# Decode attention with grouped heads on one core: 8 MB loads with 64 KB rows, K transposed in place, and the last V slots with V as stationary operand

## The chip, the cores and the metric

The kernel runs on one core of one Trainium2 chip. The metric is device microseconds (us) of one execution, lower is better; a verdict of "same" means within 2%.

Engine names in the profile: PE is TensorE (matmuls), PEld its weight loads, DVE is VectorE, ACT is ScalarE, POOL is GpSimd, SP is the engine whose queue issues the large loads (SPq is its sequencer). The granted clock is the share of TensorE's full clock that a profile records as allowed. L121 is line 121 of the kernel's source.

## The reference

One query token attends to 65,536 keys, with 32 query heads that share 8 key/value heads of width 128, all in bf16:

```python
B, Hq, Hkv, Sq, Sk, D = 1, 32, 8, 1, 65536, 128
k = jnp.repeat(k, rep, axis=1)          # rep = 4 query heads per K/V head
scores = jnp.einsum("bhqd,bhkd->bhqk", q, k) * D ** -0.5
p = softmax(scores, axis=-1)
out = jnp.einsum("bhqk,bhkd->bhqd", p, v)
```

K and V are 134 MB each and every byte is used once, so 268.4 MB must come in from memory. The order of the keys does not matter as long as K and V use the same one.

## The kernel before

For each of the 8 groups it loads K in four pieces of 4 MB, transposes each in blocks on DVE, multiplies with the queries on PE, takes the softmax, then loads V in four pieces of 4 MB and accumulates. K and V pieces share four buffers of 4 MB. In a piece each of the 128 partitions gets 128 keys ("slots"), which are 32 KB in a row of HBM.

```python
SL = 128; NB = 4                                   # slots per partition, pieces per group
iop = tc.tile_pool(name="iop", bufs=4)             # four 4 MB buffers
ktp = tc.tile_pool(name="ktp", bufs=3)             # transposed parts of K

def load(src, g, b, parts, name):
    t = iop.tile([P, SL, D], bf16, name=name, tag="io")
    view = src[0, g, b * KEYS:(b + 1) * KEYS, :].rearrange("(p t) d -> p t d", p=P)
    for lo, hi in parts:
        nc.sync.dma_start(out=t[:, lo:hi, :], in_=view[:, lo:hi, :])
    return t

# scores: 32 slots at a time
kt = ktp.tile([P, TS * D // 2], u32, name="kt")
nc.vector.transpose(out=kt[:, :], in_=kn[:, t0:t0 + TS, :] ... )     # cut
# eight matmuls of 512 columns on kt per 32 slots                      # cut

# the last piece of V (cut): comes in parts, its last 32 slots one by one
cut = [(0, 64), (64, 96), (96, 112), (112, 120), (120, 128)]
...
for t in range(96, 128):
    nc.tensor.matmul(out=fin[:, :], lhsT=et[:, b, o:o + H], rhs=vt[:, t, :], ...)
```

In the last loop the probabilities (4 columns) are the stationary operand, which a weight load (PEld) puts into PE first (`lhsT`), and V (128 columns) is the moving one (`rhs`), which is then multiplied with it.

## Time and profile before

| | before |
|---|---|
| median time, us (3 runs, 634.33 to 635.99) | 635.89 |
| profiled span, us | 634.2 |
| share of the span: PE, DVE, DMA queue of the large loads | 60%, 56%, 98.7% |
| a group of heads (33.55 MB), K landing to K landing, us | 77.8 |
| first data packet starts, last one ends, us | 1.76, 628.55 |
| last packet's end to the end of the span, us | 5.68 |

First, lines of the page of the kernel before. In the DMA line each digit is the busy share of the 16 DMA engines in one fortieth of the span, in tenths; below it what they moved. The q1 line gives packets, MB, and the share of the span that the packets took. The last two lines are groups of instructions: count, busy us, mean ns, idle time before them and what ended it.

```profile
span 634.2 us, 4903 instructions
...
DMA  8999999999999999999999999999999999999995
GB/s 366 430 436 433 437 434 432 429 430 429 432 430 431 430 429 432 430 429 430 429 430 430 429 432 431 432 435 430 428 431 432 427 432 430 429 432 431 434 423 217
...
q1 hardware_dynamic: 9944, 268.44, 98.7%
...
L121 PE MATMUL sc<-kt,wz 128*128 128x512 bf16 x1024 | 274.4, 426 | 139.1 <-DVE kt L112 139.0
L112 DVE STREAM_TRANSPOSE kt<-kn 128x2048 uint32<-128x2048 uint32 x128 | 284.4, 2278 | 23.7 <-DMA kn<-in_k_dram 23.7
```

No slice between the first and the last shows a pause of the DMA engines; PE and DVE wait. The same for two groups, from the windows view (window in us, length, busy us of each engine with its count of instructions, then PE's granted clock, DMA share, GB/s):

```profile
170.18:248.01 77.83, 46.95 (x263) 18.13 (x263) 43.85 (x33) 2.90 (x8) 0.00 (x0) 0.79 1.00 431
248.01:325.96 77.95, 45.01 (x263) 17.45 (x263) 43.97 (x33) 2.90 (x8) 0.00 (x0) 0.81 1.01 431
```

In 78 us PE works 46 and DVE 44, the DMA engines all of it. The chain of waits of the kernel before (share by line; then start and length of two pieces) must be read with that in mind:

```profile
by line: PE sc L121 31.7%; DMA kn<-in_k_dram 26.3%; DVE kt L112 20.6%; issue 6.5%; PE vacc L179 3.7%; DMA vt<-in_v_dram 3.4%; DMA q_in<-in_q_dram 1.3%; DVE mx L134 1.0%; ACT e L158 0.9%; DVE et L162 0.8%; PE fin L224 0.6%; PE pb L148 0.4%; 
...
381.08 24.00 DMA kn<-in_k_dram
405.10 2.32 DVE kt L112
```

It gives more than half of the span to PE and DVE, because it steps from a load back to the issue of that load, and from there to the work that freed its buffer. But a load that takes 9.7 us at 431 GB/s was issued 24 us before it landed: it stood in the queue most of that time. The work that freed its buffer could have been some 14 us later without costing anything (an estimate, 24.0 less 9.7).

The end of the kernel before, PE's instructions in time (start, busy us, line, operation, in brackets the idle time before):

```profile
623.96 1.04 PE L179 MATMUL vacc<-vt,et 128*16 128x512 bf16 x16 [3.02 <-DMA vt<-in_v_dram]
626.46 1.02 PE L179 MATMUL vacc<-vt,et 128*8 128x256 bf16 x16 [1.46 <-DMA vt<-in_v_dram]
627.71 2.72 PE L224 MATMUL fin<-vt,et 128*4 128x128 bf16 x24 [0.23 <-DMA vt<-in_v_dram]
630.22 0.63 PE L229 MATMUL fin<-vs,sel 128*4 128x128 f32 x2
630.65 1.06 PE L224 MATMUL fin<-vt,et 128*4 128x128 bf16 x8
```

The last part of V landed at 628.99 us; PE was then still busy with slots that had come earlier and ended 2.7 us later, at 631.71.

### The profile page before, as it was taken

What the parts mean: (1) busy time and instruction counts of PE and PEld (TensorE: products, weight loads), DVE (VectorE), ACT (ScalarE), POOL (GpSimd) and SP (SyncE); (2) the same over time, 40 slices, a digit from 0 to 9 for tenths busy, and PEclk for the clock granted to TensorE, in tenths of its full rate; (3) what the DMA queues carried; (4) which work ended last, traced back from release to release, by engine and by line L of the source; (5) the groups of instructions that cost most, each with busy time, mean ns of one, the idle gap of its engine ahead of it and who ended that gap; (6) DMA issues with size and microseconds to landing.
All of it is one profiled execution on the core that took longest, in us unless ns stands there. A gap on an engine that the chain in (4) does not pass through costs nothing.

```text
span 634.2 us, 4903 instructions
## 1 busy us (share of the span) xinstructions
PE 377.9 (60%) x2136; PEld 149.0 (23%) x2136; DVE 356.1 (56%) x291; ACT 24.5 (4%) x65; POOL 5.0 (1%) x7
## 2 busy tenths in 40 slices
PE   0876528864387644767357674576735677455865
PEld 0232203321132211322113221122211223122323
DVE  3886128761377704886057860578506785067841
ACT  0000100001000100001000010000100001000010
POOL 3000000000000000000000000000000000000000
PEclk9898767898679875988759877598865977769787
DMA  8999999999999999999999999999999999999995
GB/s 366 430 436 433 437 434 432 429 430 429 432 430 431 430 429 432 430 429 430 429 430 430 429 432 431 432 435 430 428 431 432 427 432 430 429 432 431 434 423 217
DMA packets 10213, 268.78 MB, mean 424 GB/s; under 512 B 1360, under 2 KB 1360, under 8 KB 1744
## 3 DMA queue, kind: packets, MB, share of 16 engines
q1 hardware_dynamic: 9944, 268.44, 98.7%
q8 instruction: 16, 0.26, 0.2%
q10 hardware_dynamic: 248, 0.04, 0.0%
q14 instruction: 5, 0.04, 0.0%
HBM read 268.47 MB, written 0.01 MB: 423 GB/s over the span
## 4 chain that ended last, share of the span: by engine, by line
PE 37%; DMA 31%; DVE 24%; issue 6%; ACT 1%; ACTq 0%; SPq 0%; DVEq 0%
PE sc L121 32%; DMA kn<-in_k_dram 26%; DVE kt L112 21%; PE vacc L179 4%; DMA vt<-in_v_dram 3%; DMA q_in<-in_q_dram 1%; DVE mx L134 1%; ACT e L158 1%; DVE et L162 1%; PE fin L224 1%; PE pb L148 0%; DVE m L140 0%; PE pt L138 0%; DVE wz L100 0%; DVE nrow L144 0%
## 5 line engine op out<-in xcount | busy, mean ns | idle before, releaser
L121 PE MATMUL sc<-kt,wz 128*128 128x512 bf16 x1024 | 274.4, 426 | 139.1 <-DVE kt L112 139.0
L112 DVE STREAM_TRANSPOSE kt<-kn 128x2048 uint32<-128x2048 uint32 x128 | 284.4, 2278 | 23.7 <-DMA kn<-in_k_dram 23.7
L121 PEld LDWEIGHTS <-wz 128*128 128x128 bf16 x1024 | 107.6, 105 | 305.1 <-issue 214.5
L179 PE MATMUL vacc<-vt,et 128*16 128x512 bf16 (+1 forms) x1024 | 90.5, 519 | 88.8 <-DMA vt<-in_v_dram 73.9
L191 DVE TENSOR_TENSOR vm<-vacc,mask 128x512 f32<-128x512 f32 x8 | 5.5, 692 | 141.6 <-PE vacc L179 141.6
L179 PEld LDWEIGHTS <-et 128*16 128x16 bf16 (+1 forms) x1024 | 34.1, 111 | 134.8 <-issue 108.3
L134 DVE TENSOR_REDUCE mx<-sc 128x1 f32<-128x512 f32 x32 | 22.2, 692 | 74.0 <-PE sc L121 74.0
L158 ACT ACTIVATE e<-sc,nmb 128x512 bf16<-128x512 f32 x32 | 21.7, 683 | 585.0 <-DVE nmb L153 584.1
L162 DVE STREAM_TRANSPOSE et<-e 128x512 bf16<-128x512 bf16 x32 | 22.1, 712 | 8.6 <-ACT e L158 8.6
L239 PE MATMUL fin<-vs,sel 128*4 128x128 f32 x14 | 3.7, 361 | 12.9 <-DVE vs L196 12.9
L196 DVE TENSOR_REDUCE vs<-vm 128x128 f32<-128x512 f32 x8 | 8.2, 1019 | 0.3
L138 PE MATMUL pt<-ident,mg 128*1 128x128 f32 x8 | 2.2, 270 | 7.9 <-DVE mg L136 7.9
L203 DVE TENSOR_SCALAR o<-fin,rl 4x128 bf16<-4x128 f32 x8 | 2.7, 339 | 6.8 <-PE fin L239 4.4
L158 ACT ACTIVATION_READ_ACCUMULATOR e<-sc,nmb 128x1 f32 x32 | 6.2, 194 | 0.0
L148 PE MATMUL pb<-one,nrow 1*128 1x1 f32 x16 | 3.0, 256 | 5.0 <-DVE nrow L144 5.0
L89 DVE STREAM_TRANSPOSE qT<-q_in 128x64 uint32<-128x64 uint32 x1 | 0.2, 245 | 8.8 <-DMA q_in<-in_q_dram 8.8
L239 PEld LDWEIGHTS fin<-vs,sel 128*4 128x4 f32 x14 | 0.6, 84 | 19.2 <-DVE vs L196 19.2
L63 POOL MEMSET wz<- 128x5120 bf16 x1 | 4.4, 4365 | 0.3 <-POOLq L255 0.3
L224 PE MATMUL fin<-vt,et 128*4 128x128 bf16 x32 | 3.8, 310 | 0.2 <-DMA vt<-in_v_dram 0.2
L140 DVE TENSOR_REDUCE m<-pt 1x4 f32<-1x128 f32 x8 | 2.2, 278 | 3.0 <-PE pt L138 3.0
L148 PEld LDWEIGHTS pb<-one,nrow 1*128 1x128 f32 x16 | 2.3, 182 | 6.5 <-DVE nrow L144 6.5
L224 PEld LDWEIGHTS <-et 128*4 128x4 bf16 x32 | 3.4, 126 | 0.8 <-issue 0.5
(25 smaller groups left out, 18.5 us busy)
## 6 DMA issues: line engine op xcount, KB each, us to landing
kn<-in_k_dram SPq DMA_DIRECT2D x31, 4096.0 KB, 32.4
vt<-in_v_dram SPq DMA_DIRECT2D x31, 4096.0 KB, 26.7
kn<-in_k_dram SPq DMA_DIRECT2D x2, 2048.0 KB, 11.9
vt<-in_v_dram SPq DMA_DIRECT2D x1, 2048.0 KB
vt<-in_v_dram SPq DMA_DIRECT2D x1, 1024.0 KB
vt<-in_v_dram SPq DMA_DIRECT2D x1, 512.0 KB, 21.8
vt<-in_v_dram SPq DMA_DIRECT2D x2, 256.0 KB
out_dram<-o ACTq DMA_DIRECT2D x7, 1.0 KB
```

The source lines that it names most:

```text
L63: nc.gpsimd.memset(wz[:, :, :, :, :], 0.0)
L112: nc.vector.transpose(out=kt[:, :], in_=kn[:, t0:t0 + TS, :].rearrange("p t d -> p (t d)").bitcast(u32),)
L121: nc.tensor.matmul(out=sc[:, :], lhsT=wz[:, g, s, w, 28 - 4 * gp:28 - 4 * gp + P], rhs=ktb[:, u:u + 16, s, :, w], start=(n == 0), stop=(n ...
L134: nc.vector.tensor_reduce(out=mx[:, b:b + 1], in_=scs[b][:, :], axis=AX.X, op=ALU.max)
L148: nc.tensor.matmul(out=pb[:, :], lhsT=nrow[:, :, :].rearrange("o x h -> o (x h)"), rhs=one[:, :], start=True, stop=True,)
L158: nc.scalar.activation(out=e[:, :], in_=scs[b][:, :], func=ACT.Exp, bias=nmb[:, :], scale=SCALE, accum_out=ls[:, b:b + 1],)
L162: nc.vector.transpose(out=et[:, b, :], in_=e[:, :])
L179: nc.tensor.matmul(out=vacc[32 * c:32 * c + 4 * ng, 0:ng * D], lhsT=et[:, b, o:o + 4 * ng], rhs=vt[:, :, :].rearrange("p (y t) d -> p y t ...
L191: nc.vector.tensor_tensor(out=vm[:, :, :], in0=vacc[:, :].rearrange("p (y d) -> p y d", d=D), in1=mask[:, :, :], op=ALU.mult,)
L196: nc.vector.tensor_reduce(out=vs[:, :], in_=vm[:, :, :].rearrange("p y d -> p d y"), axis=AX.X, op=ALU.add)
L224: nc.tensor.matmul(out=fin[:, :], lhsT=et[:, b, o:o + H], rhs=vt[:, t, :], start=(t == 96), stop=(t == 127),)
L239: nc.tensor.matmul(out=fin[:, :], lhsT=sel[:, :], rhs=vs[:, :], start=True, stop=True)
```

## The change

The intent is a faster DMA stream: half as many rows, each twice as long. Three 8 MB buffers need 192 KB of each partition, so everything else shrinks: K is transposed inside its own buffer, the query weights are kept for two groups rather than eight (written by GpSimd), a mask becomes a per-partition factor. The last V slots change the roles of their operands so that PE should have less to do after the last landing. The diff, cut:

```diff
-SL = 128
-NB = 4
+SL = 256
+NB = 2
...
-    iop = ctx.enter_context(tc.tile_pool(name="iop", bufs=4))
-    ktp = ctx.enter_context(tc.tile_pool(name="ktp", bufs=3))
+    iop = ctx.enter_context(tc.tile_pool(name="iop", bufs=3))
...
-            kt = ktp.tile([P, TS * D // 2], u32, name="kt")
-            nc.vector.transpose(
-                out=kt[:, :],
-                in_=kn[:, t0:t0 + TS, :].rearrange("p t d -> p (t d)").bitcast(u32),
-            )
+            part = kn[:, t0:t0 + TS, :].rearrange("p t d -> p (t d)")
+            nc.vector.transpose(out=part.bitcast(u32), in_=part.bitcast(u32))
...
-                cut = [(0, 64), (64, 96), (96, 112), (112, 120), (120, 128)]
-                for t in range(96, 128):            # V moving, 32 slots
...
+    cuts = [0, 128, 192, 224, 240, 248, 256]
+    vs = collect()
+    for t in range(192, 240):                       # V stationary, 48 slots
+        nc.tensor.matmul(
+            out=oT[:, :], lhsT=vt[:, t, :], rhs=et[:, 3, o:o + H], start=(t == 192), stop=(t == 239)
+        )
+    nc.vector.tensor_copy(out=oTs[:, :], in_=oT[:, :])
+    nc.tensor.matmul(out=fin[:, :], lhsT=sel[:, :], rhs=vs[:, :], start=True, stop=False)
+    nc.tensor.matmul(out=fin[:, :], lhsT=oTs[:, :], rhs=ident[:, :], start=False, stop=False)
+    for t in range(240, 256):                       # V moving, 16 slots
+        nc.tensor.matmul(
+            out=fin[:, :], lhsT=et[:, 3, o:o + H], rhs=vt[:, t, :], start=False, stop=(t == 255)
+        )
```

More of the change, by code (lines that the diff above doesn't have):

```diff
@@ L14 @@
 D = 128
-SL = 128
-NB = 4
+SL = 256
+NB = 2
+NS = 4
 G = 8
@@ L39 @@
     const = ctx.enter_context(tc.tile_pool(name="const", bufs=1))
-    iop = ctx.enter_context(tc.tile_pool(name="iop", bufs=4))
-    ktp = ctx.enter_context(tc.tile_pool(name="ktp", bufs=3))
-    ep = ctx.enter_context(tc.tile_pool(name="ep", bufs=2))
+    iop = ctx.enter_context(tc.tile_pool(name="iop", bufs=3))
+    ep = ctx.enter_context(tc.tile_pool(name="ep", bufs=1))
     st = ctx.enter_context(tc.tile_pool(name="st", bufs=2))
@@ L47, with load @@
     pfn = ctx.enter_context(tc.tile_pool(name="pfn", bufs=1, space=bass.MemoryType.PSUM))
-    def load(src, g, b, parts, name):
+    def load(src, g, b, cuts, name):
         t = iop.tile([P, SL, D], bf16, name=name, tag="io")
         view = src[0, g, b * KEYS:(b + 1) * KEYS, :].rearrange("(p t) d -> p t d", p=P)
-        for lo, hi in parts:
+        for lo, hi in zip(cuts, cuts[1:]):
             nc.sync.dma_start(out=t[:, lo:hi, :], in_=view[:, lo:hi, :])
         return t
+    first = load(k, 0, 0, [0, SL], "kn")
     q_in = const.tile([P, D], bf16)
@@ L59 @@
         nc.scalar.dma_start(out=q_in[32 * a:32 * a + 32, :], in_=q[0, :, 0, :])
-    first = load(k, 0, 0, [(0, 64), (64, 128)], "kn")
-    wz = const.tile([P, G, 2, 2, WB], bf16)
-    nc.gpsimd.memset(wz[:, :, :, :, :], 0.0)
+    wz = [const.tile([P, 2, 2, WB], bf16, name=f"wz{i}") for i in range(2)]
+    for w in wz:
+        nc.gpsimd.memset(w[:, :, :, :], 0.0)
     ident = const.tile([P, P], fp32)
@@ L67 @@
     nc.vector.memset(one[:, :], 1.0)
-    ones = const.tile([P, 512], fp32)
-    nc.vector.memset(ones[:, :], 1.0)
     sel = const.tile([P, H], fp32)
@@ L82 @@
     )
-    mask = const.tile([P, 4, D], fp32)
-    for y in range(4):
-        nc.vector.tensor_scalar_mul(out=mask[:, y, :], in0=ones[:, 0:D], scalar1=sely[:, y:y + 1])
+    vacc = pva.tile([P, 4, D], fp32)
+    nc.vector.memset(vacc[:, :, :], 0.0)
     qT = const.tile([P, 2, 32], u32)
@@ L94, with weights, scores @@
     )
-    for a in range(4):
-        rows = slice(32 * a, 32 * a + 32)
-        c0 = 28 + 32 * a
-        for s in range(2):
-            for w in range(2):
-                nc.vector.tensor_copy(
-                    out=wz[rows, :, s, w, c0:c0 + H], in_=qTb[rows, s, :, :, w]
-                )
-    vacc = pva.tile([P, 512], fp32)
-    nc.vector.memset(vacc[:, :], 0.0)
-    def scores(g, kn):
+    def weights(g):
+        w = wz[g % 2]
+        for a in range(4):
+            rows = slice(32 * a, 32 * a + 32)
+            c0 = 28 + 32 * a
+            nc.gpsimd.tensor_copy(
+                out=w[rows, :, :, c0:c0 + H],
+                in_=qTb[rows, :, g, :, :].rearrange("p s h w -> p s w h"),
+            )
+        return w
+    def scores(kn, w, t_lo):
         sc = psc.tile([P, 512], fp32, name="sc")
         n = 0
-        for t0 in range(0, SL, TS):
-            kt = ktp.tile([P, TS * D // 2], u32, name="kt")
-            nc.vector.transpose(
-                out=kt[:, :],
-                in_=kn[:, t0:t0 + TS, :].rearrange("p t d -> p (t d)").bitcast(u32),
-            )
-            ktb = kt[:, :].bitcast(bf16).rearrange("p (t s i w) -> p t s i w", s=2, i=32, w=2)
+        for t0 in range(t_lo, t_lo + 128, TS):
+            part = kn[:, t0:t0 + TS, :].rearrange("p t d -> p (t d)")
+            nc.vector.transpose(out=part.bitcast(u32), in_=part.bitcast(u32))
+            ktb = part.rearrange("p (t s i w) -> p t s i w", s=2, i=32, w=2)
             for u in range(0, TS, 16):
-                gp = (t0 + u) // 16
+                gp = (t0 - t_lo + u) // 16
                 for s in range(2):
-                    for w in range(2):
+                    for e in range(2):
                         nc.tensor.matmul(
                             out=sc[:, :],
-                            lhsT=wz[:, g, s, w, 28 - 4 * gp:28 - 4 * gp + P],
-                            rhs=ktb[:, u:u + 16, s, :, w],
+                            lhsT=w[:, s, e, 28 - 4 * gp:28 - 4 * gp + P],
+                            rhs=ktb[:, u:u + 16, s, :, e],
                             start=(n == 0),
@@ L131, in softmax @@
     def softmax(g, scs):
-        mx = st.tile([P, NB], fp32, name="mx")
-        for b in range(NB):
+        mx = st.tile([P, NS], fp32, name="mx")
+        for b in range(NS):
             nc.vector.tensor_reduce(out=mx[:, b:b + 1], in_=scs[b][:, :], axis=AX.X, op=ALU.max)
@@ L153, in softmax @@
         nc.vector.tensor_copy(out=nmb[:, :], in_=pb[:, :])
-        ls = st.tile([P, NB], fp32, name="ls")
-        et = ep.tile([P, NB, 512], bf16, name="et")
-        for b in range(NB):
-            e = ep.tile([P, 512], bf16, name="e")
+        ls = st.tile([P, NS], fp32, name="ls")
+        et = ep.tile([P, NS, 512], bf16, name="et")
+        for b in range(NS):
             nc.scalar.activation(
-                out=e[:, :], in_=scs[b][:, :], func=ACT.Exp, bias=nmb[:, :], scale=SCALE,
+                out=et[:, b, :], in_=scs[b][:, :], func=ACT.Exp, bias=nmb[:, :], scale=SCALE,
                 accum_out=ls[:, b:b + 1],
             )
-            nc.vector.transpose(out=et[:, b, :], in_=e[:, :])
-        pl = pms.tile([H, NB], fp32, name="pl", tag="misc")
+            nc.vector.transpose(out=et[:, b, :], in_=et[:, b, :])
+        pl = pms.tile([H, NS], fp32, name="pl", tag="misc")
         nc.tensor.matmul(out=pl[:, :], lhsT=sel[:, :], rhs=ls[:, :], start=True, stop=True)
@@ L171, with wcol, wide @@
     started = set()
-    def wide(g, b, et, vt, gp0, ng, last=False):
+    def wcol(t):
+        return (t % 16) * 32 + 4 * (t // 16)
+    def wide(g, b, et, vt, t_lo, last=False):
+        bank, gp0 = (b * SL + t_lo) // 128, (t_lo % 128) // 16
+        vv = vt[:, t_lo:t_lo + 64, :].rearrange("p (y t) d -> p y t d", t=16)
         for tt in range(16):
             c = tt % 4
-            key = (g, c)
             o = tt * 32 + 4 * gp0
             nc.tensor.matmul(
-                out=vacc[32 * c:32 * c + 4 * ng, 0:ng * D],
-                lhsT=et[:, b, o:o + 4 * ng],
-                rhs=vt[:, :, :].rearrange("p (y t) d -> p y t d", t=16)[:, gp0:gp0 + ng, tt, :],
-                start=key not in started,
+                out=vacc[32 * c:32 * c + 16, :, :],
+                lhsT=et[:, bank, o:o + 16],
+                rhs=vv[:, :, tt, :],
+                start=(g, c) not in started,
                 stop=last and tt >= 12,
@@ L186, in wide, with collect @@
             )
-            started.add(key)
-    def collect(g):
-        vm = st.tile([P, 4, D], fp32, name="vm")
-        nc.vector.tensor_tensor(
-            out=vm[:, :, :], in0=vacc[:, :].rearrange("p (y d) -> p y d", d=D),
-            in1=mask[:, :, :], op=ALU.mult,
-        )
-        vs = st.tile([P, D], fp32, name="vs")
-        nc.vector.tensor_reduce(
-            out=vs[:, :], in_=vm[:, :, :].rearrange("p y d -> p d y"), axis=AX.X, op=ALU.add
-        )
+            started.add((g, c))
+    def collect():
+        vs = st.tile([P, D], fp32, name="vs")
+        nc.vector.tensor_scalar_mul(out=vs[:, :], in0=vacc[:, 0, :], scalar1=sely[:, 0:1])
+        for y in range(1, 4):
+            nc.vector.scalar_tensor_tensor(
+                out=vs[:, :], in0=vacc[:, y, :], scalar=sely[:, y:y + 1], in1=vs[:, :],
+                op0=ALU.mult, op1=ALU.add,
+            )
         return vs
@@ L205, in finish @@
         store.dma_start(out=out[0, g * H:(g + 1) * H, 0, :], in_=o[:, :])
-    pend = None
     for g in range(G):
+        w = weights(g)
         scs = []
         for b in range(NB):
-            kn = first if (g, b) == (0, 0) else load(k, g, b, [(0, 128)], "kn")
-            scs.append(scores(g, kn))
+            kn = first if (g, b) == (0, 0) else load(k, g, b, [0, SL], "kn")
+            scs.append(scores(kn, w, 0))
+            scs.append(scores(kn, w, 128))
         et, rl = softmax(g, scs)
-        for b in range(NB):
-            if g == G - 1 and b == NB - 1:
-                cut = [(0, 64), (64, 96), (96, 112), (112, 120), (120, 128)]
-                vt = load(v, g, b, cut, "vt")
-                wide(g, b, et, vt, 0, 4)
-                wide(g, b, et, vt, 4, 2, last=True)
-                fin = pfn.tile([H, D], fp32, name="fin")
-                vs = collect(g)
-                for t in range(96, 128):
-                    o = (t % 16) * 32 + 4 * (t // 16)
-                    nc.tensor.matmul(
-                        out=fin[:, :], lhsT=et[:, b, o:o + H], rhs=vt[:, t, :],
-                        start=(t == 96), stop=(t == 127),
-                    )
-                    if t == 119:
-                        nc.tensor.matmul(
-                            out=fin[:, :], lhsT=sel[:, :], rhs=vs[:, :], start=False, stop=False
-                        )
-            else:
-                vt = load(v, g, b, [(0, 128)], "vt")
-                wide(g, b, et, vt, 0, 4)
-                wide(g, b, et, vt, 4, 4, last=(b == NB - 1))
-        if g < G - 1:
-            vs = collect(g)
@@ L238 @@
+        end = g == G - 1
+        for b in range(NB - end):
+            vt = load(v, g, b, [0, SL], "vt")
+            for t_lo in range(0, SL, 64):
+                wide(g, b, et, vt, t_lo, last=(b == NB - 1 and t_lo == SL - 64))
+        if not end:
+            vs = collect()
             fin = pfn.tile([H, D], fp32, name="fin")
             nc.tensor.matmul(out=fin[:, :], lhsT=sel[:, :], rhs=vs[:, :], start=True, stop=True)
-        finish(g, fin, rl)
+            finish(g, fin, rl)
+    g, b = G - 1, NB - 1
@@ new lines @@
+    cuts = [0, 128, 192, 224, 240, 248, 256]
+    vt = load(v, g, b, cuts, "vt")
+    for t_lo in (0, 64, 128):
+        wide(g, b, et, vt, t_lo, last=(t_lo == 128))
+    vs = collect()
+    oT = pms.tile([P, H], fp32, name="oT", tag="misc")
+    for t in range(192, 240):
+        o = wcol(t - 128)
+        nc.tensor.matmul(
+            out=oT[:, :], lhsT=vt[:, t, :], rhs=et[:, 3, o:o + H], start=(t == 192), stop=(t == 239)
+        )
+    oTs = st.tile([P, H], fp32, name="oTs")
+    nc.vector.tensor_copy(out=oTs[:, :], in_=oT[:, :])
@@ L244 @@
+    fin = pfn.tile([H, D], fp32, name="fin")
+    nc.tensor.matmul(out=fin[:, :], lhsT=sel[:, :], rhs=vs[:, :], start=True, stop=False)
+    nc.tensor.matmul(out=fin[:, :], lhsT=oTs[:, :], rhs=ident[:, :], start=False, stop=False)
+    for t in range(240, 256):
+        o = wcol(t - 128)
+        nc.tensor.matmul(
+            out=fin[:, :], lhsT=et[:, 3, o:o + H], rhs=vt[:, t, :], start=False, stop=(t == 255)
+        )
+    finish(g, fin, rl)
 _INS = ['q', 'k', 'v']
```

## The prediction

> **What bounds the kernel now.** The DMA stream. The slice view shows DMA busy at 9 or more in all slices but the first and last, at 430 GB/s; the windows view gives each group of heads (33.55 MB) 77.8 us from 14.6 to 559.2 us, at DMA share 1.00 and 431 GB/s. The Trainium skill, page "DMA: Bandwidth & Descriptors", section "Where 436 GB/s comes from", puts the ceiling at 435.2 GB/s; the trace agrees to 1%. PE (60%) and DVE (56%) have room; the chain of waits names them only because it follows when buffers come free, some 17 us before the queue needs them (issue to landing is 27 to 32 us, a 4 MB load takes 9.7). At the ends: about 2.5 us before the first byte, and some 6 us after the last landing: PE at granted clock 0.50 on the last slots (24 matmuls in 2.72 us from 627.71, two f32 matmuls 0.43, eight matmuls 0.87), the scaling 0.34, the store about 2.4.
>
> **The stream.** Bytes stay. In the trace's packet records a 16 KB row took 611 ns (median) on its DMA engine, a 32 KB row 1216, a semaphore packet 9. So a row costs about 6 ns beside its bytes. Each engine moves 512 rows of 32 KB; with 64 KB rows 256, which saves about 1.5 us, and half the semaphore packets 0.3 us. If a 64 KB row is cut in two, only the 0.3 us remain. Saving: 0.3 to 1.8 us, all on the critical path.
>
> **Do three buffers starve the queue?** Estimate: an 8 MB load takes 19.5 us; load n needs load n-3 consumed within 39 us of landing. K: eight transposes of 2.27 us = 18.2 us on DVE, no longer held up by three kt buffers; PE, at 0.27 us a matmul, ends 2 to 5 us later. So K is free 21 to 24 us after landing; softmax takes 5 us, 8 MB of V 6 us. The tightest slack is about 15 us. In-place transposes wait only for their own region: the trace already shows reads waiting for just their piece (the cut last V load: 619.04, 623.96, 626.46, 627.71). The stream should stay unbroken. Fewer constants, weights on GpSimd, a later first transpose (22 us instead of 13) and q arriving later are off the path.
>
> **The tail.** 48 slots with V stationary, f32 matmuls, then 16 slots in the old form (16 x 0.11 = 1.8 us). Before, 32 in the old form. If a V-stationary slot costs 0.06 us, the end is as before; if 0.11 like the old ones, PE ends about 2.5 us later. I take +0.7 us.
>
> **Sum.** 635.9 - 1.8 + 0.7 = 634.8 us, range 631 to 638.5. Faster by over 2% 0.02, within 2% 0.95, slower by over 2% 0.03. Faster than 623 is nearly excluded: the bytes alone take 617 us at the ceiling.
>
> **What would show it.** Stream: group windows of 77.4 to 77.7 us, DMA share 1.00; 64 KB packets of about 2.43 us, DMA packet count near 5,000. Buffers: SP issues 10 us or more before the running load ends; no slice under 425 GB/s. Tail: from last V landing to the end of the last matmul 3 us before, 3 to 5.5 after.
>
> **What would make it wrong.** A tracker that orders transposes behind matmuls of the same tile (K then takes 38 us and the stream stalls some 18 us per group, over 10% slower); 64 KB packets at another rate; in-place transposes slower than 2.27 us; a much cheaper tail.

## The result, and the profile after

The changed kernel took 633.0 us (median of 4 runs, 632.85 to 633.37), the kernel before 635.31 us (now 4 runs), ratio 0.9966 with a 95% interval of 0.9948 to 0.9983. A ratio is the mean time of one kernel's fast runs over that of the other's of the same rounds, so not quite the ratio of the medians. Three later repeats on three chips gave 0.9950, 0.9955 and 0.9952, by medians 3.1, 2.7 and 3.1 us. So the gain is 2.3 to 3.1 us, 0.3 to 0.5%: small, but clear of the noise.

The page of the changed kernel, the same lines as before:

```profile
span 631.0 us, 4882 instructions
...
DMA  9999999999999999999999999999999999999995
GB/s 400 404 461 420 441 404 457 428 434 453 408 457 407 458 411 450 415 446 428 433 436 428 433 432 429 437 428 437 424 442 420 445 425 440 433 432 429 436 407 231
...
q1 hardware_dynamic: 5336, 268.44, 98.6%
...
L116 PE MATMUL sc<-kn,wz 128*128 128x512 bf16 x1024 | 262.0, 410 | 170.9 <-DVE kn L110 170.6
L110 DVE STREAM_TRANSPOSE kn<-kn 128x2048 uint32<-128x2048 uint32 x128 | 282.5, 2274 | 80.2 <-DMA kn<-in_k_dram 80.2
```

The DMA line has no gap: three buffers are enough. The GB/s line now swings between 400 and 461, which is not a stall: bytes are counted by whole packets, a packet is 64 KB now, and most engines start their packets together (11 of 16 within 0.4 us, from 201.1 us on). The in-place transposes take 2.27 us as the others did. Two groups in the windows view of the changed kernel:

```profile
179.20:256.64 77.44, 44.20 (x263) 17.49 (x263) 43.22 (x35) 2.78 (x8) 0.76 (x4) 0.83 1.00 434
256.64:334.08 77.44, 45.56 (x263) 18.04 (x263) 43.22 (x35) 2.78 (x8) 0.76 (x4) 0.76 1.00 434
```

A group takes 77.44 us where it took 77.83 and 77.95 (most others before 77.8), at the same DMA share of 1.00: the engines are as busy, and get more through. In each of the two profiles one of the six K-to-K intervals is longer by 1.4 us (79.1 before, 78.9 after); what that is stays open, and it is the same on both sides.

The packet records put the whole difference in place:

| from the packet records, us | before | after |
|---|---|---|
| first data packet starts | 1.76 | 1.76 |
| last data packet ends | 628.55 | 625.93 |
| length of the stream | 626.79 | 624.17 |
| from there to the end of the span | 5.68 | 5.10 |
| packet of a 32 KB row, of a 64 KB row, median ns | 1216, - | 1216, 2421 |

Of the 3.2 us between the profiled spans, 2.6 are stream and 0.6 tail. The chain of waits of the changed kernel:

```profile
by line: DVE kn L110 42.0%; DMA kn<-in_k_dram 40.8%; DMA vt<-in_v_dram 5.3%; PE sc L116 4.5%; DMA q_in<-in_q_dram 4.4%; issue 0.8%; PE fin L243 0.3%; PE oT L233 0.2%; ACTq L60 0.2%; DVE vs L192 0.2%; PE vacc L178 0.2%; DVE mx L129 0.1%; PE 
...
2.13 27.97 DMA q_in<-in_q_dram
...
374.00 39.01 DMA kn<-in_k_dram
413.01 0.02 issue
413.03 17.67 DVE kn L110 x8
```

Two things are to be seen. The K load is issued 39 us before it lands and takes 19.4, so the buffer came free some 19 us early. And the four small q loads, 8 KB each, took 28 us (8.5 before): they share the DMA engines with the 8 MB loads, which now hold an engine for 2.4 us per packet. The runs with shorter rows, told below, bear this out, with all else kept: the transpose of q began at 30.2 us here, at 18.1 with 32 KB rows and at 9.4 with 8 KB rows. The late q moved the first transposes to 31 us.

The end of the changed kernel, PE's instructions in time:

```profile
621.34 1.04 PE L178 MATMUL vacc<-vt,et 128*16 128x512 bf16 x16 [0.90 <-DMA vt<-in_v_dram]
623.99 0.59 PE L239 MATMUL fin<-vs,sel 128*4 128x128 f32 x2 [1.61 <-DVE vs L192]
624.51 1.44 PE L233 MATMUL oT<-et,vt 128*128 128x4 bf16 x48
626.21 0.59 PE L240 MATMUL fin<-ident,oTs 128*4 128x128 f32 x2 [0.26 <-DVE oTs L237]
626.59 1.91 PE L243 MATMUL fin<-vt,et 128*4 128x128 bf16 x16
```

The 48 slots with V stationary took 1.44 us, 30 ns each at granted clock 0.50; the 16 old-style slots took 1.91 us, 119 ns each. The last part of V landed at 626.37, so all of the 1.91 us lie behind it, and PE ended 2.1 us after it. The cheap slots hardly depend on the clock: in the run with 32 KB rows below, 48 of them took 1.35 us at granted clock 1.00, 28 ns each.

### The profile page after: what moved, and what is told of

Its sections match the earlier page's. It is cut to its first block, busy times and chain, and to the rows that moved or that the text cites. A ratio compares the mean times of both kernels' runs of the same rounds, so it can differ in the third digit from the quotient of the medians.

```text
span 631.0 us, 4882 instructions
## 1 busy us (share of the span) xinstructions
PE 362.8 (57%) x2154; PEld 145.2 (23%) x2154; DVE 347.3 (55%) x287; ACT 23.6 (4%) x65; POOL 7.9 (1%) x40
## 4 chain that ended last, share of the span: by engine, by line
DMA 51%; DVE 43%; PE 5%; issue 1%; ACTq 0%; SPq 0%; DVEq 0%
DVE kn L110 42%; DMA kn<-in_k_dram 41%; DMA vt<-in_v_dram 5%; PE sc L116 5%; DMA q_in<-in_q_dram 4%; PE fin L243 0%; PE oT L233 0%; ACTq L60 0%; DVE vs L192 0%; PE vacc L178 0%; DVE mx L129 0%; PE fin L239 0%; PE fin L240 0%; DVE vs L190 0%; DVE o L200 0%
## 5 line engine op out<-in xcount | busy, mean ns | idle before, releaser
L116 PE MATMUL sc<-kn,wz 128*128 128x512 bf16 x1024 | 262.0, 410 | 170.9 <-DVE kn L110 170.6
L110 DVE STREAM_TRANSPOSE kn<-kn 128x2048 uint32<-128x2048 uint32 x128 | 282.5, 2274 | 80.2 <-DMA kn<-in_k_dram 80.2
L116 PEld LDWEIGHTS <-wz 128*128 128x128 bf16 x1024 | 104.4, 102 | 326.6 <-issue 195.9
L178 PE MATMUL vacc<-vt,et 128*16 128x512 bf16 x1008 | 88.6, 526 | 46.2 <-DMA vt<-in_v_dram 44.4
L178 PEld LDWEIGHTS <-et 128*16 128x16 bf16 x1008 | 33.9, 116 | 96.6 <-issue 86.1
L152 ACT ACTIVATE et<-sc,nmb 128x512 bf16<-128x512 f32 x32 | 21.5, 685 | 586.7 <-DVE nmb L148 586.7
L156 DVE STREAM_TRANSPOSE et<-et 128x512 bf16<-128x512 bf16 x32 | 21.7, 711 | 7.1 <-ACT et L152 7.1
L99 POOL COPY wz<-qT 32x16 bf16<-32x16 bf16 x32 | 6.1, 190 | 445.5 <-PE sc L116 415.9
L192 DVE SCALAR_TENSOR_TENSOR vs<-vacc,sely,vs 128x128 f32<-128x128 f32 x24 | 8.4, 351 | 0.9
L152 ACT ACTIVATION_READ_ACCUMULATOR et<-sc,nmb 128x1 f32 x32 | 6.5, 203 | 0.0
```

What stands on the lines that cost most here:

```text
L99: nc.gpsimd.tensor_copy(out=w[rows, :, :, c0:c0 + H], in_=qTb[rows, :, g, :, :].rearrange("p s h w -> p s w h"),)
L110: nc.vector.transpose(out=part.bitcast(u32), in_=part.bitcast(u32))
L116: nc.tensor.matmul(out=sc[:, :], lhsT=w[:, s, e, 28 - 4 * gp:28 - 4 * gp + P], rhs=ktb[:, u:u + 16, s, :, e], start=(n == 0), stop=(n == 31),)
L152: nc.scalar.activation(out=et[:, b, :], in_=scs[b][:, :], func=ACT.Exp, bias=nmb[:, :], scale=SCALE, accum_out=ls[:, b:b + 1],)
L156: nc.vector.transpose(out=et[:, b, :], in_=et[:, b, :])
L178: nc.tensor.matmul(out=vacc[32 * c:32 * c + 16, :, :], lhsT=et[:, bank, o:o + 16], rhs=vv[:, :, tt, :], start=(g, c) not in started, stop= ...
```

## The experiments

**Theory.** A row costs about 10 ns on its DMA engine beside its bytes; half as many rows save the 2.6 us of the stream. **Rivals.** (a) The size and number of the loads pays, not the row. (b) The spacing of the rows in HBM matters. (c) The new tail is the gain. (d) Compute or buffers matter, as the chain of waits suggests. The changed kernel ran again beside each set. The edits are shown shortened; text after a `#` in them is a remark or stands for code left out.

> The changed kernel once more, on the same chip as the next three, as their base. Repeats its result: 2.0 to 2.6 us under the kernel before (ratio 0.9959 to 0.9969), 64 KB packets of 2421 ns median, first packet at 1.8 us, last packet ends near 625.9 us.

It took 632.91 us (kernel before 636.05, ratio 0.9950, interval 0.9937 to 0.9964): half a microsecond more gain than I had expected, in the kernel before's time rather than in its own (632.91 against 633.0).

**Rows of 32 KB in one 8 MB load.** Two 32 KB rows per partition from two places, still one load:

```diff
-view[:, lo:hi, :]                                   # "(p t) d -> p t d"
+src[...].rearrange("(h p t) d -> p h t d", h=2, p=P)   # one load, two 32 KB rows per partition
```

> The changed kernel, still one 8 MB load at a time into three buffers, but each load takes its 64 KB per partition as two 32 KB rows from two places of HBM (the keys are only permuted, the result stays right). Theory (the row is what pays: about 10 ns per packet beside the bytes): packets of 32 KB at 1216 ns, about 248 more per engine, so the stream is 248 x 11 ns = 2.7 us longer than the changed kernel's; time 635.5 to 636, level with the kernel before within 0.1% or so once its new tail is counted. Rival (the size and number of loads pays, or the new tail): level with the changed kernel, ratio to before 0.9966.

635.33 us (just under the 635.5 to 636 expected), 2.42 over the changed kernel on the same chip; packets of 1216 ns; the stream 626.52 us, against 624.38 for the changed kernel beside it. Two groups in the windows view of this run:

```profile
102.05:179.84 77.79, 43.87 (x263) 17.46 (x263) 43.22 (x35) 2.78 (x8) 0.76 (x4) 0.83 1.00 431
179.84:257.60 77.76, 45.62 (x263) 17.94 (x263) 43.21 (x35) 2.78 (x8) 0.76 (x4) 0.79 1.00 431
```

The group is back at 77.8 us and 431 GB/s with 8 MB loads, three buffers, in-place transposes and the new tail all kept. Rival (a) falls.

**Two 4 MB loads side by side.** Each load from slot 0 to 128 and 128 to 256:

```diff
-load(k, g, b, [0, SL], "kn")
+load(k, g, b, [0, 128, 256], "kn")                 # V the same
```

> The changed kernel with each 8 MB load issued as two 4 MB loads side by side in the buffer (32 KB rows at a 64 KB pitch). Theory (rows): as with two 32 KB rows in one load, plus 31 more semaphore packets of 9 ns per engine = 0.3 us: 2.9 to 3.2 us over the changed kernel. Rival (number of loads): the whole gain is lost here but not in the run with 32 KB rows in one load. Rival (pitch of the rows in HBM): this one differs from that run by more than 0.3 us.

636.18 us, 3.3 over the changed kernel. The stream is 626.47 us, the same as with 32 KB rows in one load, though the rows lie at another pitch and there are 31 more loads: rival (b) falls, and the 0.3 us I had put on the extra semaphore packets are not to be seen. A group in this run:

```profile
169.91:247.69 77.78, 45.47 (x263) 17.97 (x263) 43.62 (x35) 2.78 (x8) 0.76 (x4) 0.83 1.00 431
```

By the criterion, more than 0.3 us between the two runs, the times alone would have spoken for rival (b), and the estimate of 2.9 to 3.2 us was nearly met for another reason than the one given. The 0.85 us between the two times are in the tail (5.82 against 4.72 us after the last packet). In this run's profile PE's clock was at 0.50 for the last 10 us, in the other's for the last 5. I did not isolate what sets that.

**Rows of 8 KB.** As the 32 KB run, with h=8.

> The changed kernel with one 8 MB load at a time made of 8 KB rows. Theory (a fixed cost per packet): 8 KB packets took 313 ns in the cut last load of the kernel before, so 64 KB take 8 x 313 = 2504 ns in place of 2421; 248 x 83 ns = 20.6 us over the changed kernel, time about 653. Rival (engine rate does not depend on the row, only on load size): within 1 us of the changed kernel.

650.62 us (4 runs), 17.7 over the changed kernel; the estimate was 20.6. Two groups in the windows view:

```profile
184.04:263.72 79.68, 44.50 (x263) 17.65 (x263) 43.22 (x35) 2.78 (x8) 0.76 (x4) 0.78 1.01 421
263.72:343.41 79.69, 44.78 (x263) 17.73 (x263) 43.22 (x35) 2.79 (x8) 0.76 (x4) 0.80 1.01 420
```

The DMA share reads 1.01: recorded packet times overlap a little when packets are short, so summing them counts too much (645.9 us per engine in this run, in a stream of 641.6). The intervals are the safer measure. In a group each engine moves 32 times 64 KB:

| row | K-to-K interval, us | per 64 KB and engine, ns | over the 64 KB row, per extra row, ns |
|---|---|---|---|
| 64 KB | 77.44 | 77.44 / 32 = 2420 | |
| 32 KB | 77.78 | 2431 | 11 / 1 = 11 |
| 8 KB | 79.69 | 2490 | 70 / 7 = 10 |

One cost per row, 10 to 11 ns, fits all three. Single intervals vary (two of six in the first repeat of the changed kernel are 77.8 us), so the whole streams are a second measure: against the mean of four profiles of the changed kernel, 624.17 us, the 32 KB rows cost 9.5 ns each (2.35 us, 248 rows more per engine) and the 8 KB rows 9.9 (17.4 us, 1768 more). Without the row cost 64 KB would take 2410 ns, which on 16 engines is 435 GB/s. The Trainium skill's "DMA: Bandwidth & Descriptors", section "Where 436 GB/s comes from", states 435.2 GB/s as the ceiling; this agrees. The same section says that for loads from HBM the memory side, about 358 GB/s, binds first; here, with one core at work, it did not (434 measured). So, by this fit, the changed kernel's stream is 0.4% from what longer rows could only approach.

**The tail, both ways.** First the second base, then the changed kernel with the old tail, then the kernel before with the new one.

> The changed kernel again, as base of the next three on the same chip: ratio to before 0.9959 to 0.9969.

632.97 us (ratio 0.9955, again a little more gain than expected).

```diff
-    for t in range(192, 240): oT ... V stationary        # and copy, f32 matmul, 16 slots V moving
+    wide over slots 192 to 224; for t in range(224, 256): fin ... V moving
```

> The changed kernel with the old handling of the last 64 slots (two of the four rows wide, 32 slots with V moving). Theory: the new tail gives 0.5 to 0.7 us of the gain (last packet's end to the span's end 5.7 before, 5.1 after), the stream is the same; so 0.5 to 0.7 us over the changed kernel, last-packet-to-end 5.6 to 5.8. Rival (the new tail gives nothing, the 0.6 is chance): level with the changed kernel. My prediction said the new tail would cost 0.7 us: then this would be 0.7 us faster.

632.67 us (631.88 to 632.96), 0.3 under the changed kernel, with ranges that overlap (632.75 to 633.15 there): the theory's 0.5 to 0.7 us are not there. PE in this run:

```profile
625.02 2.09 PE L241 MATMUL fin<-vt,et 128*4 128x128 bf16 x24 [0.65 <-DMA vt<-in_v_dram]
626.90 0.63 PE L245 MATMUL fin<-vs,sel 128*4 128x128 f32 x2
627.33 1.06 PE L241 MATMUL fin<-vt,et 128*4 128x128 bf16 x8
```

PE ends at 628.39, 2.1 us after its last landing, as with the new tail. The same 24 matmuls that took 2.72 us in the kernel before took 2.09 here; there the clock was at 0.50 for all of them, here it was at 0.91 in the microsecond in which they began.

```diff
-                wide(g, b, et, vt, 4, 2, last=True)      # then 32 slots V moving
+                for t in range(64, 112): oT ... V stationary   # then copy, f32 matmul, 16 slots V moving
```

> The kernel before with the new tail alone (48 slots with V stationary, then 16 with V moving). Theory: 0.5 to 0.7 us under the kernel before, ratio 0.9989 to 0.9992, packets still 1216 ns for 32 KB. If the tail were the gain: ratio 0.9966.

635.7 us against 635.63, ratio 0.9999 (0.9987 to 1.0012). Rival (c) falls, and so does my first reading that the tail gave 0.6 us. The tail as built pays in one place and gives it back in another: 48 slots became cheap, but the copy, one more f32 matmul and 16 slots of 119 ns come after them, and all of the 16 slots stand behind the last landing. One part of the tail was not swapped: DVE's collecting of the wide sums, which the new tail's first matmul waits for, took 1.74 us with the old mask (625.10 to 626.84 in the last run) and 1.50 with the per-partition factor (622.43 to 623.93 in the changed kernel), and each kernel kept its own.

**All 64 last slots with V stationary.**

```diff
-    for t in range(192, 240):
+    for t in range(192, 256):
-    for t in range(240, 256): fin ... V moving
```

> The changed kernel with all 64 last slots with V stationary; the 16 slots that took 1.83 us (115 ns each, after the last landing) take 16 x 30 ns = 0.5 us, mostly before the last landing; the copy and the two f32 matmuls (0.16 + 0.6) move behind the last landing. Estimate: last landing 626.4, 8 slots 0.25, copy 0.2, f32 matmuls 0.6, so PE ends at about 627.6 in place of 628.5: 0.8 to 1.0 us under the changed kernel. If a V-stationary slot costs 110 ns beside a waiting DMA, no gain.

632.18 us (632.14 to 632.30), 0.8 under the changed kernel on the same chip and with ranges that don't touch; ratio to the kernel before 0.9943. PE:

```profile
624.60 1.65 PE L233 MATMUL oT<-et,vt 128*128 128x4 bf16 x56
626.51 0.37 PE L233 MATMUL oT<-et,vt 128*128 128x4 bf16 x8 [0.27 <-DMA vt<-in_v_dram]
627.14 0.59 PE L240 MATMUL fin<-ident,oTs 128*4 128x128 f32 x2 [0.25 <-DVE oTs L237]
```

PE now waits for the last landing rather than having work left over, and ends 1.3 us after it. As an improvement of the new tail this is clear. Against the old tail in the same kernel (632.67, 631.88 to 632.96) it is 0.5 us by the medians, but the ranges overlap: that it beats the old tail is likely, not shown.

**Buffers, the chain of waits, and a last bit of tail.** The third base:

> The changed kernel as base of the next three on the same chip: 632.6 to 633.3 us.

632.84 us (ratio 0.9952).

```diff
-    iop = ctx.enter_context(tc.tile_pool(name="iop", bufs=3))
+    iop = ctx.enter_context(tc.tile_pool(name="iop", bufs=2))
```

> The changed kernel with two 8 MB buffers in place of three. Worked out from its trace: a K load is consumed 19.7 us after it lands and the next load takes 19.4 us, so with two buffers the first V load of a group can be issued only about when the second K load has landed, and issue, first packet and completion then leave the DMA engines idle some 2 us; all other loads still come in time. So one bubble of 1.5 to 2.5 us per group, a K-to-K interval of 79 to 80 us in place of 77.45, and 12 to 20 us over the changed kernel. Rival (the kernel needs deep queueing, each load loses): several bubbles a group, over 40 us. Rival (buffers don't matter): level.

680.44 us, 47.6 over the changed kernel, and a K-to-K interval of 82.4 us: I was off by more than a factor of two, and the result fell where I had put the rival, several bubbles a group and over 40 us. The page, and two pieces of the chain:

```profile
DMA  9949999899997999979999799997999979998995
GB/s 380 430 182 430 379 438 437 355 392 417 434 433 317 426 433 430 433 314 433 430 433 433 318 425 430 433 433 318 422 434 433 430 325 421 434 433 383 371 381 240
```

```profile
247.56 31.56 DMA kn<-in_k_dram
...
329.76 31.79 DMA kn<-in_k_dram
```

The dips come once per group. In the group from 279 us the packet records show the engines running dry from 296.1 us, none of them moving data from 298.1 to 299.8, while the first V load waits for the first K buffer, and again, less deeply, from 319.9 to 321.3, when the second V load was issued only as the first one ended. As a mean of the 16 engines the two dips are 3.2 and 0.5 us; I had put 1.5 to 2.5 on the first and had not counted the second. They are 3.7 of the 5.0 us by which the interval grew; I did not trace the rest. Eight groups at 5.0 us and about 8 us at the start, where the first K waits for q and nothing is queued behind, make the 47.6. So the third buffer is needed, and what it buys is a queue that is never empty. It also shows what a real buffer limit looks like in the DMA line.

```diff
-    first = load(k, 0, 0, [0, SL], "kn")
-    nc.scalar.dma_start(out=q_in[...], in_=q[...])       # four of them
+    nc.sync.dma_start(out=q_in[...], in_=q[...])         # four of them, ahead of the first K load
+    first = load(k, 0, 0, [0, SL], "kn")
```

> The changed kernel with the four small q loads issued ahead of the first K load on the same queue. q then lands by about 5 us instead of 30, and the first transposes start about 22.5 to 25 us instead of 31. Theory (the DMA stream alone sets the time): the four issues of 0.44 us delay the first K packet by 1.3 to 1.8 us and the whole kernel is 1.3 to 1.8 us slower, though all compute of the first group runs 6 to 8 us earlier. Rival (the chain of waits, which runs through the q load with 4.4% of the span, names a real limit): several us faster.

634.39 us, 1.55 over the changed kernel. VectorE's first K transposes in this run:

```profile
24.61 13.28 DVE L110 STREAM_TRANSPOSE kn<-kn 128x2048 uint32<-128x2048 uint32 x6 [19.83 <-DMA kn<-in_k_dram]
```

They begin 6.5 us earlier than in the changed kernel, and the kernel is slower by what the first K packet lost (3.61 us in place of 1.77, less 0.2 us in a shorter stream). Rival (d) falls for a kernel with three buffers: the 4.4% that the chain gave to the q load were worth nothing. The DMA stream, and the tail behind its last packet, set the time.

```diff
-    oTs in f32; lhsT=oTs[:, :], rhs=ident[:, :]           # all 64 slots with V stationary, as above
+    oTs in bf16; lhsT=oTs[:, :], rhs=identb[:, :]         # one bf16 pass
```

> All 64 last slots with V stationary, and the turn back of their sum as one bf16 matmul with a bf16 identity in place of an f32 one in two passes. The two passes took 0.59 us; one bf16 pass should take 0.2 to 0.3, so 0.3 to 0.4 us under the f32 version (632.18 then), i.e. 1.0 to 1.2 us under the changed kernel, and it is the fastest of all; last packet to end 3.8 to 3.9 us. Result still correct.

632.15 us, correct; 0.7 under the changed kernel, level with the f32 version of another chip (632.18). The pass took 0.27 us in place of 0.59, and last packet to end was 3.92 us in place of 4.23, but the times do not show it. The version that beats both kernels is the one with all last slots stationary, in either form, at about 632.2 us, 0.6% under the kernel before.

## Why the prediction was right, and where it was off

The time of 633.0 us lies in the range of 631 to 638.5, and the call "within 2%, the stream stays bound by DMA" held. That takes little: the range also holds the kernel before (635.3), and the gain measured was more than double the 1.1 us predicted. What held is the mechanism, a DMA-bound stream shortened by fewer rows; the sizes of its two terms did not, and both erred to the same side. Point by point:

- *DMA stream bounds the kernel, stays unbroken with three buffers*: right. DMA share 1.00, no empty slice. The stated slack of 15 us was 19 in later groups, but only about 8 in the first: q came at 30 us, so K0 and K1 were consumed late, and the first K load of the next group was issued at 71.0 us, 8 us before its turn (79.2, worked out as 1.76 + four loads of 19.4). My marker "10 us or more" failed there.
- *Group windows of 77.4 to 77.7 us*: 77.44. *64 KB packets of about 2.43 us*: 2.42. *Packet count near 5,000*: 5,605. *No slice under 425 GB/s*: wrong marker; slices go down to 400 with the engines full, since packets are counted whole.
- *A row costs about 6 ns beside its bytes, saving 1.5 us*: mis-sized. I had taken 2 x 611 - 1216 from the medians of 16 and 32 KB packets, a difference of numbers that carry an error of some ns each (in the trace of the changed kernel the 16 KB median is 614, and the same sum gives 12). The runs with 32 and 8 KB rows give about 10 ns (9.5 to 11), so 248 fewer rows per engine save 2.4 to 2.7 us, and the stream was shorter by 2.6. The page "DMA: Bandwidth & Descriptors", section "Measured (HBM→SBUF, 128 partitions, SWDGE, issued from GpSimd)", gives about 10.5 ns per packet for small transfers on another issuing path; this case shows the same size for rows of 8 to 64 KB; that it is the same cost is not shown.
- *Tail +0.7 us*: wrong in its term and in its sign against the profile. I had put a V-stationary slot at 60 to 110 ns; it took 30. The tail of the first profile was 0.6 us shorter, yet swapping the tails both ways moved the time by -0.3 and +0.1 us, and my marker, 3 to 5.5 us from the last landing to the last matmul's end, came out at 2.1 (2.7 before): as built, it is worth nothing that these runs can resolve.
- *Sum*: -1.8 + 0.7 = -1.1 us predicted, -2.3 to -3.1 measured. The stream accounts for 2.6; a remainder of up to 0.5 us goes, in the profiles, with a higher PE clock at the end when loads are 8 MB. That was seen, not isolated; the collecting step, 0.2 us shorter, may be part of it.

## What to carry to other kernels

When the DMA engines are full in every slice, count what each engine does per row: the bytes at the ceiling plus about 10 ns, and lengthen rows only until that term is small (3.2% of the stream at 8 KB, 0.9% at 32 KB, 0.4% at 64 KB here). Do not take the chain of waits at its word in such a kernel; compare the time from issue to landing with the time the bytes take, and what exceeds it is slack. In a tail behind the last landing, give the large operand to the stationary side when the other has few columns, and carry that through to the last slot (here 0.8 us less than stopping at three quarters of the slots; against not starting, the times leave it open).

## What the Trainium skill lacked or had wrong

- "DMA: Bandwidth & Descriptors", section "Why small descriptors are slow (HBM only)", names a fixed cost per packet, but works it out only for a descriptor of 256 bytes. Here a cost of 10 to 11 ns per row was still measurable between 32 and 64 KB rows: 77.78 against 77.44 us per group, 2.4 us of the kernel.
- The same page, section "Queues, rings and completion order", says that an engine switches between queues at packet boundaries, but not what long packets do to a small load on another queue: the four 8 KB loads of q landed after 8.5 us beside rows of 16 and 32 KB and after 28.0 us beside rows of 64 KB (15.7 us in the same kernel with 32 KB rows).
- "TensorE: Matmul & The Clock Gate", section "Weight-path perf modes — Fast Weight Load (FWL) and DoubleRow", has no figure for a stream of bf16 matmuls with 128 stationary and 4 moving columns. Here it ran at 30 ns per pair of weight load and matmul at granted clock 0.50 (28 ns at 1.00), against 119 ns at 0.50 with the operands exchanged (4 stationary, 128 moving).
